# The last dense half of expert 0 as two more pairs of the Strassen passes

## The chip, the cores and the metric

The kernel runs on one core of a Trainium2 chip. The metric is the device time of one execution in microseconds; for the kernel before it is the median of three runs. TensorE does the matmuls into PSUM, VectorE, ScalarE and GpSimd the elementwise work, and SyncE issues nearly all transfers from one queue. In the profile they are called PE (PEld: its weight loads), DVE, ACT, POOL and SP.

## What is computed

Strided sparse attention over 4 batches, 8 heads, 576 positions and a head size of 64 gives x of 2304 tokens by 512. A mixture of 8 experts follows, in which every token goes through every expert; the gate is a Sinkhorn iteration over all tokens, so that no gate is known before the last token's logits.

```python
logits = x @ w_gate
P = np.exp(logits - logits.max())
for _ in range(8):
    P /= P.sum(1, keepdims=True) + 1e-09
    P /= P.sum(0, keepdims=True) + 1e-09
    P *= N / E
for e in range(E):
    h = np.maximum(x @ w1[e], 0.0)        # 512 -> 1024
    out += P[:, e:e + 1] * (h @ w2[e])    # 1024 -> 512
```

All of it is in float32. The kernel splits each operand of the experts' matmuls into a high and a low part and takes three products (high by high, high by low, low by high).

## The kernel before

**Dense phase.** Expert 0 is computed without the gate, since the gate isn't known yet. Its 1024 hidden columns are two F halves (`u` = 0 and 1, `UPE` = 2) of four tiles of 128 each (`FH` = 4, `ft`). A slot is one group of tokens by one `ft`: `layer1` makes twelve matmuls into `ph` and `rectify` the high part on ACT and the low part on DVE; `layer2` of the slot before follows and accumulates `y` over the four `ft`. The first half has 9 groups of 256 tokens, that is slots 0 to 35, and the attention's steps lie in slots 0 to 26. The second half has groups of 512, 512, 256, 512 and 512 tokens, slots 36 to 55. After the first half `y` is copied by ACT into `acc` (18 tiles of 128 tokens in `acc` and `tail`), after the second it is added by DVE, and the tiles from 6 on are stored to `yd` in DRAM. The layers 2 of the last two slots (`rest`) stand in step 0 of the passes.

**What lies beside the dense phase.** `store_x` writes x to `xd` in DRAM. `beside` gives the slots from 27 on their other work by a table: the logits (`gate_logits`, tile `pl`; `gate_transpose`, `pg`), the start of the gate (`pm`) and eight Sinkhorn rounds (`sinkhorn`: DVE row sums and a scaling, column sums `g8`, the matmul `pc` on PE, a second scaling on DVE); the sums of x for all three passes (`build_s`, read from `xd`, added on POOL, split by ACT and DVE, stored to `sd`); the operands of the first two pairs (`prep_w1`); and the scaling of `acc` by expert 0's gate (`scale`, on ACT).

**The passes.** The other experts are computed in three passes over 768 tokens each, by Strassen's scheme with seven products in the first layer: `step(g)` works on pair `g`, that is one tile of 128 hidden columns of either half of an expert, with x's blocks and their sums (`x11`, `x12`, `x22`, `s1` to `s4`) loaded into `reg`, over x's old place. There are `NK` = 28 pairs per pass. Pass 1 prepares the weights (`prep_w1` on POOL and ACT, `prep_w2` and `w2_sums` on DVE and ACT) and stores them to `wd` and `w2d`, and its second layer is ordinary (`second`, 36 matmuls); passes 2 and 3 load them back and have seven products in the second layer as well (`second_strassen`, 42 matmuls), but for one and two pairs at their ends. `step(g)` ends pair g-1: its last two products come first (`finish_first`), then five products of pair g, then the second layer of g-1.

Every engine runs its instructions in the order in which the code records them. So a wait of one instruction holds up all that stand behind it on its engine, and a DMA that waits for its buffer holds up the DMAs behind it on SP.

Of the kernel before, what the change touches and what calls it, by code (L numbers as in the profile page):

```python
# [55 lines left out]
def kernel(  # L56
# [35 lines left out]
    stacks = {"tail": ExitStack()}  # L92
    tail_p = stacks["tail"].enter_context(tc.tile_pool(name="tail", bufs=1))
# [17 lines left out]
    LATE = range(12, 16)  # L111
    EARLY = [t for t in range(HEAD, NTT) if t not in LATE]
    acc = big.tile([P, HEAD + len(LATE), D], F32, name="acc")
# [12 lines left out]
    tail = tail_p.tile([P, len(EARLY), D], F32, name="tail")  # L126
# [27 lines left out]
    plain = [(u, ft, which) for u in range(UPE) for ft in range(FH) for which in range(2)]  # L154
    plain[: 2 * FH] = sorted(plain[: 2 * FH], key=lambda x: x[2])
    plain[2 * FH :] = sorted(plain[2 * FH :], key=lambda x: (x[0], x[1] + 1.5 * x[2]))
# [288 lines left out]
    def layer2(u, c, ft, only=None):  # L445
# [8 lines left out]
        for i in range(nt) if only is None else only:  # L454
# [6 lines left out]
            if ft == FH - 1:  # L461
                t = c0 // P + i
                if t in EARLY:
                    o = tail[:, EARLY.index(t), :]
                else:
                    o = acc[:, t if t < HEAD else HEAD + t - LATE[0], :]
# [27 lines left out]
    for name in ("s3", "x22", "s4", "x12"):  # L494
        x_at[name] = at
        at += XN
    assert x_at["x12"] == 4 * 2 * NDT * CH and at <= 2 * NDT * NT
# [10 lines left out]
    NK = (E - 1) * FP  # L508
# [18 lines left out]
    def build_s(p, k):  # L527

        st = pools["sb"].tile([P, 4, 2, TN], F32, tag="sx", name=f"sx_{p}_{k}", bufs=2)
        t0 = 2 * TN * p  # L530
        for i, (dh, th) in enumerate(((0, 0), (0, 1), (1, 1), (1, 0))):
            nc.sync.dma_start(
                st[:, i], xd[:, :, k + 2 * dh, t0 + TN * th : t0 + TN * (th + 1)]
            )
        yield
        x, s = st[:, :, 0, :], st[:, :, 1, :]
        for i in (0, 2):
            nc.gpsimd.tensor_tensor(
# [759 lines left out]
```

## Time and profile before

| | us |
|---|---|
| median of 3 runs | 1563.97 (1562.67 to 1566.0) |
| the profiled execution | 1562.6 |
| its span, first to last instruction | 1560.8 |
| busy: TensorE | 1545.4 |
| busy: VectorE | 1270.2 |
| busy: GpSimd | 970.6 |
| busy: ScalarE | 536.6 |

The busy time of an engine counts the time in which at least one of its instructions runs, waits for a shared port among it. The granted clock of TensorE is full throughout. In the span the first F half's slots begin near 31 us, the second half's at 190.8, step 0 at 289.0, and the second layer of pass 2's first pair at 743.

### The profile page before, as it was taken

The numbers are of one execution on the slowest core, as the hardware profiler recorded it, in microseconds if no ns is written. First come the engines' busy times: TensorE is split into PE (matmuls) and PEld (weight loads), VectorE is DVE, ScalarE is ACT, GpSimd is POOL, SyncE is SP. The second block draws the span as 40 slices with busy tenths as digits, with TensorE's granted clock in tenths as the row PEclk, the third lists the DMA queues.
The fourth block names the chain that finished last, engine by engine and source line by source line (L and its number), as shares of the span: only waits on it lengthen the run. The fifth ranks groups of instructions, "written<-read, shape, count | busy, mean of one in ns | idle before, by whom it ended". The sixth has DMA issues, their size and how long they took to land.

```text
span 1560.8 us, 25458 instructions
## 1 busy us (share of the span) xinstructions
PE 1545.4 (99%) x9146; PEld 1452.1 (93%) x9146; DVE 1270.2 (81%) x2457; ACT 536.6 (34%) x1261; POOL 970.6 (62%) x899
## 2 busy tenths in 40 slices
PE   8999999999999999999999999999999999999999
PEld 6888888899999999989999999999999999999997
DVE  5655266699999999997688888888868888888887
ACT  6665322334343434342432222222232332222221
POOL 4221456365665565561777777777867877877874
PEclk9999999999999999999999999999999999999999
DMA  7553667988898888887866666666756766766762
GB/s 223 193 164 110 232 212 272 326 314 323 319 331 314 333 315 327 305 324 279 330 270 264 276 261 243 271 267 245 286 213 271 292 257 253 283 246 249 280 239 92
DMA packets 116766, 413.82 MB, mean 265 GB/s; under 512 B 9280, under 2 KB 63392, under 8 KB 102688
## 3 DMA queue, kind: packets, MB, share of 16 engines
q1 hardware_dynamic: 116496, 412.06, 70.0%
q8 instruction: 73, 1.20, 0.3%
q14 instruction: 53, 0.43, 0.1%
q10 hardware_dynamic: 144, 0.13, 0.0%
HBM read 275.27 MB, written 136.89 MB: 264 GB/s over the span
## 4 chain that ended last, share of the span: by engine, by line
PE 96%; DVE 1%; DMA 1%; POOL 0%; ACT 0%; issue 0%; DVEq 0%; POOLq 0%; ACTq 0%
PE p L827 25%; PE bb L697 17%; PE yg L726 16%; PE ba L697 11%; PE bc L697 11%; PE ph L424 6%; PE y L457 6%; PE tp L289 1%; DMA qk<-in_qkv 1%; PE sc L241 1%; PE pv L302 1%; PE pl L352 1%; PE sc L224 0%; PE pv L316 0%; PE tr L857 0%; POOL sm L277 0%
## 5 line engine op out<-in xcount | busy, mean ns | idle before, releaser
L835 DVE TENSOR_TENSOR total<-p,total 128x384 f32<-128x384 f32 x714 | 371.6, 557 | 0.8 <-PE p L827 0.8
L697 PE MATMUL bb<-reg 128*128 128x384 f32 x1512 | 304.3, 335 | 1.1 <-DVE u L750 0.7
L697 PEld LDWEIGHTS bb<-reg 128*128 128x128 f32 x1512 | 266.0, 188 | 4.1 <-DVE u L750 1.0
L697 PE MATMUL ba<-reg 128*128 128x384 f32 x1008 | 201.8, 334 | 0.6 <-DVE u L750 0.6
L697 PE MATMUL bc<-reg 128*128 128x384 f32 x1008 | 201.8, 334 | 0.0
L750 DVE TENSOR_TENSOR u<-bb,m 128x384 f32<-128x384 f32 x168 | 93.3, 555 | 106.3 <-PE bb L697 102.9
L808 ACT ACTIVATE a<-u 128x384 fp32r<-128x384 f32 x106 | 55.7, 526 | 359.4 <-DVE u L802 359.3
L697 PEld LDWEIGHTS ba<-reg 128*128 128x128 f32 x1008 | 177.2, 188 | 1.0 <-DVE u L750 0.9
L697 PEld LDWEIGHTS bc<-reg 128*128 128x128 f32 x1008 | 177.4, 188 | 0.0
L884 POOL TENSOR_TENSOR s1t<-m,u 128x384 f32<-128x384 f32 x53 | 53.9, 1017 | 189.3 <-DVE m L802 189.3
L733 DVE SCALAR_TENSOR_TENSOR acc<-yg,gate,acc 128x512 f32<-128x512 f32 x186 | 131.4, 741 | 9.6 <-PE yg L726 9.6
L726 PE MATMUL yg<-w2t,h 128*128 128x512 f32 x504 | 117.1, 390 | 0.0
L726 PE MATMUL yg<-w2b,h 128*128 128x512 f32 x504 | 117.1, 390 | 0.0
L827 PE MATMUL p<-s,w2b 128*128 128x384 f32 x648 | 116.7, 334 | 0.0
L424 PE MATMUL ph<-reg,w 128*128 128x256 f32 (+1 forms) x672 | 114.6, 318 | 0.0
L827 PEld LDWEIGHTS p<-s,w2b 128*128 128x128 f32 x648 | 112.7, 188 | 0.0
L827 PE MATMUL p<-s,w2t 128*128 128x384 f32 x624 | 112.3, 334 | 0.0
L457 PE MATMUL y<-w2t,h 128*128 128x512 f32 x432 | 111.0, 398 | 1.3 <-DVE acc L470 0.9
L726 PEld LDWEIGHTS yg<-w2b,h 128*128 128x128 f32 x504 | 94.4, 188 | 19.1
L726 PEld LDWEIGHTS yg<-w2t,h 128*128 128x128 f32 x504 | 94.4, 188 | 19.1
L812 POOL TENSOR_TENSOR a<-u,a 128x384 fp32r<-128x384 f32 x106 | 109.0, 1029 | 0.0
L827 PEld LDWEIGHTS p<-s,w2t 128*128 128x128 f32 x624 | 108.5, 188 | 0.0
(147 smaller groups left out, 2847.3 us busy)
## 6 DMA issues: line engine op xcount, KB each, us to landing
reg<-wd SPq DMA_DIRECT2D x52, 1792.0 KB
wd<-reg SPq DMA_DIRECT2D x28, 1792.0 KB
w2b<-w2d SPq DMA_DIRECT2D x25, 1792.0 KB
w2t<-w2d SPq DMA_DIRECT2D x24, 1792.0 KB
w2d<-w2b SPq DMA_DIRECT2D x14, 2048.0 KB
w2d<-w2t SPq DMA_DIRECT2D x14, 2048.0 KB
raws<-in_w SPq DMA_DIRECT2D x72, 256.0 KB
sx<-xd SPq DMA_DIRECT2D x24, 384.0 KB
```

The costliest lines, as they stand in the source:

```text
L241: nc.tensor.matmul(scs[j][:m, i, :m], t[sl, i * m : (i + 1) * m], t[sl, nq + i * m : nq + (i + 1) * m], start=True, stop=True,)
L424: nc.tensor.matmul(ph[:, :n], w[:, i, dt, :], xv(x, dt, c0, n), start=(first and len(taken) == 1 and i + x == 0), stop=(len(taken) == NDT ...
L457: nc.tensor.matmul(y, h[:, a, i * P : (i + 1) * P], w[:, b, :], start=(ft == 0 and first), stop=(ft == FH - 1 and a == 1),)
L697: nc.tensor.matmul(out[:, :TN], w[:, i, k, :], xops[x][:, xi, k, :], start=(start and n == 0), stop=(n == 5), skip_group_check=True,)
L726: nc.tensor.matmul(y, hg[g, i // 3, f][:, a, o : o + P], w[:, b, f, :], start=(f == 0 and a + b == 0), stop=(f == 1 and a == 1),)
L733: nc.vector.scalar_tensor_tensor(acc[:, i, :], y, gate[:, t, e : e + 1], acc[:, i, :], op0=ALU.mult, op1=ALU.add)
L750: nc.vector.tensor_tensor(o, bank[:, :TN], s, op=ALU.add)
L808: nc.scalar.activation(t[:, 0], src, AF.Copy)
L812: nc.gpsimd.tensor_tensor(t[:, 1], src, t[:, 0].bitcast(F32), op=ALU.subtract)
L827: nc.tensor.matmul(y[:, :TN], w[:, b, wi, d, :], h[:, a, :], start=(a + b == 0), stop=(a == 1),)
L835: nc.vector.tensor_tensor(o, y[:, :TN], o, op=ALU.add)
L884: nc.gpsimd.tensor_tensor(s1, m1, u3, op=ALU.add)
```

## The change

The second F half of expert 0 leaves the dense phase. Its four tiles of 128 hidden columns become two more pairs, pair (0, 2) and (1, 3), with expert index 0, so `NK` is 30; `f_at` gives the place of their columns in W1 and W2. The dense phase has slots 0 to 35 alone. With it go `tail`, the additions of `y` on DVE and the weight loads of that half; ACT copies each `y` to `acc` or, from tile 6 on, to one of four staging tiles that are stored to `yd`.

The work that stood beside the second half has new places:

- the logits' first three groups stand in slots 6 and 7, 13 and 14, 20 and 21, the other two in slots 27 and 28, the start of the gate in 28 and 29, and the Sinkhorn rounds in slots 29 to 35; the last round's matmul and second scaling stand after step 0, and the scaling of `acc` behind them
- the sums of x are built in pieces of 128 tokens instead of 384. Those of pass 1 (six pieces) are read from `reg` itself in slots 8 to 22; those of passes 2 and 3 (twelve pieces) are built in steps 3 to 27 of pass 1 (`later_sums`), one `next` per step, with the subtraction on POOL instead of DVE
- the raw weights of the first pair are loaded in slot 9 and prepared in slots 23 to 26, those of the second are loaded in slot 27 and prepared in slots 29 to 32

```diff
-    plain = [(u, ft, which) for u in range(UPE) for ft in range(FH) for which in range(2)]
...
+    plain = [(0, ft, which) for which in range(2) for ft in range(FH)]
...
-                if u == 0:
+                if t < HEAD:
+                    nc.scalar.activation(acc[:, t, :], y, AF.Copy)
+                else:
+                    o = acc[:, HEAD + t % STAGE, :]
                     nc.scalar.activation(o, y, AF.Copy)
-                else:
-                    nc.vector.tensor_tensor(o, y, o, op=ALU.add)
-                    if t >= HEAD:
-                        nc.sync.dma_start(yd[:, t - HEAD, :], o)
+                    nc.sync.dma_start(yd[:, t - HEAD, :], o)
...
-    NK = (E - 1) * FP
+    FE = (UPE - 1) * FH // 2
+    NK = (E - 1) * FP + FE
...
-            groups.append((p, 1 + k // FP, k % FP, k))
+            groups.append((p, (1 + k // FP) % E, k % FP, k))
...
+    def f_at(g, fh):
+        _, e, j, _ = groups[g]
+        return (FP * fh + j if e else FH + FE * fh + j) * P
...
+        t0 = 2 * TN * p + P * th
+        if p:
+            for i, (dh, t) in enumerate(((0, t0), (0, t0 + TN), (1, t0 + TN), (1, t0))):
+                nc.sync.dma_start(st[:, i], xd[:, :, k + 2 * dh, t : t + P])
+            yield
...
+        else:
+            for o, t in ((x[:, 0:4:3], t0), (x[:, 1:3], t0 + TN)):
+                ci, c = divmod(t, CH)
+                hi, lo = (
+                    chunk(ci)[:, i, k : k + 3 : 2, c : c + P].bitcast(F32) for i in range(2)
+                )
+                nc.gpsimd.tensor_tensor(o, hi, lo, op=ALU.add)
...
+        engine = nc.gpsimd if p else nc.vector
+        engine.tensor_tensor(so[:, 1], s, so[:, 0].bitcast(F32), op=ALU.subtract)
...
+    for n, (k, th) in enumerate((k, th) for k in range(2) for th in range(3)):
+        w = build_s(0, k, th)
+        for i in ((8, 9, 9), (10, 11, 11), (12, 15, 15), (16, 17, 17), (18, 19, 19), (19, 22, 22))[n]:
+            at(i, next, w, None)
+    w1_first = [prep_w1(g) for g in range(2)]
+    for g, i, pieces_at in ((0, 9, (23, 24, 25, 26)), (1, 27, (29, 30, 31, 32))):
+        at(i, load_w1g, g)
+        for n in pieces_at:
+            at(n, next, w1_first[g], None)
+    for i, name in (
+        (23, "x11"), (24, "s2"), (25, "s1"), (32, "x12"), (32, "s3"), (33, "x22"), (35, "s4"),
+    ):
+        at(i, load_x, 0, name)
+    at(27, load_w1g, 2)
+    at(33, load_w2g, 0)
+    for i, n in ((27, 1), (28, 2), (29, 1), (30, 1), (31, 1), (32, 1), (33, 1), (34, 1), (35, 1)):
+        for _ in range(n):
+            at(i, next, gat, None)
+    ahead_of_second = {28: 2, 29: 1, 35: 1}
...
+        for _ in range(ahead_of_second.get(slot, 0)):
+            next(gat, None)
...
+        elif slot in (6, 7, 13, 14, 20, 21):
             next(gat)
...
+            if g == 0:
+                assert next(gat, gat) is gat
+                for i in range(HEAD):
+                    scale(0, i)
             if g == 4:
                 gate_rows()
+            if g > 2:
+                next(later, None)
```

**PE around the last slots.** Before, a Sinkhorn round's `pc` has a whole slot of 512 tokens (`ph`, then four tiles of `y`) behind it; the rows end with step 0's first products (`ba`, `bb`):

```order
L389 MATMUL pc_3525<-g_7_3477,ones 128x8
L424 MATMUL ph_1536_2_3531<-reg,w_1_2_2697 128x512 x12
L457 MATMUL y_1536_0_3495<-w2t,h_1536_1_3492 128x512 x3
L457 MATMUL y_1536_1_3496<-w2t,h_1536_1_3492 128x512 x3
L457 MATMUL y_1536_2_3497<-w2t,h_1536_1_3492 128x512 x3
L457 MATMUL y_1536_3_3498<-w2t,h_1536_1_3492 128x512 x3
L424 MATMUL ph_1536_3_3564<-reg,w_1_3_2738 128x512 x12
L697 MATMUL ba_3609<-reg 128x384 x6
L697 MATMUL bb_3610<-reg 128x384 x6
```

After, in slots 34 and 35 and the start of step 0:

```order
L420 MATMUL ph_2048_2_2858<-reg,w_0_2_312 128x256 x12
L453 MATMUL y_2048_0_2834<-w2t,h_2048_1_2831 128x512 x3
L453 MATMUL y_2048_1_2835<-w2t,h_2048_1_2831 128x512 x3
L385 MATMUL pc_2880<-g_4_2856,ones 128x8
L420 MATMUL ph_2048_3_2893<-reg,w_0_3_365 128x256 x12
L385 MATMUL pc_2909<-g_5_2891,ones 128x8
L385 MATMUL pc_2923<-g_6_2920,ones 128x8
L692 MATMUL ba_2957<-reg 128x384 x6
L692 MATMUL bb_2958<-reg 128x384 x6
L692 MATMUL bc_2959<-reg 128x384 x6
L692 MATMUL ba_2957<-reg 128x384 x6
L453 MATMUL y_2048_0_2834<-w2t,h_2048_2_2871 128x512 x3
```

Slot 35 has a first layer alone, and the pc of two rounds follow each other behind it; `y` of the last two slots comes four products later, as before.

**ACT from the last slots to step 1.** Before, with the scaling of `acc` (`acc<-acc,gate`) in slots 54 and 55, the `w2b` rows of step 0 and the copy `m_1` of step 1:

```order
L1090 ACTIVATE acc<-acc,gate 128x512 x3
L439 ACTIVATE h_1536_3_3577<-ph_1536_3_3564 128x512
L1090 ACTIVATE acc<-acc,gate 128x512 x3
L181 ACTIVATE reg<-raws 128x256
L919 ACTIVATE m_0_3606<-ba_3609 128x384
L758 ACTIVATE h_0_3638<-ba_3609 128x384
L685 ACTIVATE w2b<-raws 128x1024
L653 ACTIVATE w2b<-w2sum_3643 128x1024
L758 ACTIVATE h_0_3688<-u_0_3608 128x384
L758 ACTIVATE h_0_3706<-m_0_3606 128x384
L758 ACTIVATE h_0_3715<-u_0_3607 128x384
L919 ACTIVATE m_1_3719<-ba_3722 128x384
```

After, from step 0's copy `m_0` to step 1's first weights (`ra`):

```order
L914 ACTIVATE m_0_2954<-ba_2957 128x384
L753 ACTIVATE h_0_2986<-ba_2957 128x384
L680 ACTIVATE w2b<-raws 128x1024
L648 ACTIVATE w2b<-w2sum_2991 128x1024
L463 ACTIVATE acc<-y_2048_0_2834 128x512
L463 ACTIVATE acc<-y_2048_1_2835 128x512
L753 ACTIVATE h_0_3020<-u_0_2956 128x384
L1111 ACTIVATE acc<-acc,gate 128x512 x6
L753 ACTIVATE h_0_3050<-m_0_2954 128x384
L753 ACTIVATE h_0_3059<-u_0_2955 128x384
L914 ACTIVATE m_1_3063<-ba_3066 128x384
L177 ACTIVATE reg<-ra_2590 128x512
```

All six scalings stand behind step 0's last relu, ahead of the two relus with which step 1 begins and of its copy `m_1`; two copies of `y` are new in step 0.

**SP around the raw weights of the second pair.** Before, from the load of `x12` into `reg` to the raw weights of the third pair:

```order
L574 DMA reg<-xd 128x4x384
L634 DMA wd<-reg 128x3584
L594 DMA raws<-in_w 128x2x128 x4
L562 DMA sd<-so_1_0_3367 128x2x384 x2
L472 DMA yd<-tail 128x512 x4
L562 DMA sd<-so_1_2_3368 128x2x384 x2
L594 DMA ra_3517<-in_w 128x2x128 x2
L594 DMA rb_3518<-in_w 128x2x128 x2
```

After, from the last two stores of x (slot 26) to the loads of slot 32:

```order
L149 DMA xd<-reg 1024x1x512
L149 DMA xd<-reg 1024x1x256
L629 DMA wd<-reg 128x3584
L589 DMA raws<-in_w 128x2x128 x4
L589 DMA ra_2590<-in_w 128x2x128 x2
L589 DMA rb_2591<-in_w 128x2x128 x2
L464 DMA yd<-acc 128x512 x4
L629 DMA wd<-reg 128x3584
L569 DMA reg<-xd 128x4x384
L565 DMA reg<-sd 128x1536
```

The raw weights (`raws<-in_w`) stand behind the last two stores of x and the store of the first pair's operands (`wd`); before, a load of x and that store stood ahead of them.

## Rows read from the trace of the kernel before

**Rows 1.** Page, part 1: busy us, share of the span, instructions of each engine.
```profile
PE 1545.4 (99%) x9146; PEld 1452.1 (93%) x9146; DVE 1270.2 (81%) x2457; ACT 536.6 (34%) x1261; POOL 970.6 (62%) x899
```

**Rows 2.** Timeline of PE, first F half: start us, us, instructions [idle before <-releaser].
```profile
53.55 0.56 PE L224 MATMUL sc<-qk 64*64 64x96 f32 x16 [1.18 <-DMA qk<-in_qkv]
...
156.45 1.59 PE L424 MATMUL ph<-reg,w 128*128 128x256 f32 x12
157.88 1.55 PE L457 MATMUL y<-w2t,h 128*128 128x512 f32 x6
...
162.63 1.99 PE L352 MATMUL pl<-reg,wgs 128*128 128x512 f32 x8
```

**Rows 3.** Timeline of PE, second F half.
```profile
206.01 2.88 PE L424 MATMUL ph<-reg,w 128*128 128x512 f32 x12
208.73 2.89 PE L457 MATMUL y<-w2t,h 128*128 128x512 f32 x12
...
240.88 1.62 PE L457 MATMUL y<-w2t,h 128*128 128x512 f32 x6 [0.94 <-DVE acc L470]
```

**Rows 4.** Timeline of PE, steps 0 and 1 and the second layer of the next.
```profile
288.96 1.22 PE L697 MATMUL ba<-reg 128*128 128x384 f32 x6
...
301.23 1.31 PE L697 MATMUL bb<-reg 128*128 128x384 f32 x6 [0.68 <-DVE u L750]
...
308.62 8.36 PE L726 MATMUL yg<-w2b,h 128*128 128x512 f32 x36
...
324.13 8.36 PE L726 MATMUL yg<-w2t,h 128*128 128x512 f32 x36
```

**Rows 5.** Timeline of PE, two pairs of pass 2, first product of each.
```profile
765.75 1.20 PE L697 MATMUL bb<-reg 128*128 128x384 f32 x6
...
780.32 1.20 PE L697 MATMUL bb<-reg 128*128 128x384 f32 x6
```

**Rows 6.** Timeline of DVE: a Sinkhorn round alone, and one beside GpSimd's sums.
```profile
211.78 0.17 DVE L391 TENSOR_SCALAR r<-pc 128x8 f32<-128x8 f32 x1
...
212.90 0.18 DVE L382 TENSOR_SCALAR g<-g 128x18 f32<-128x18 f32 x1
...
213.75 0.44 DVE L386 TENSOR_REDUCE g<-gate 128x8 f32<-128x144 f32 x1
...
258.41 0.17 DVE L391 TENSOR_SCALAR r<-pc 128x8 f32<-128x8 f32 x1 [1.53 <-PE pc L389]
...
259.53 1.36 DVE L382 TENSOR_SCALAR g<-g 128x18 f32<-128x18 f32 x1
...
262.15 0.44 DVE L386 TENSOR_REDUCE g<-gate 128x8 f32<-128x144 f32 x1
```

**Rows 7.** Timelines of SP's queue and ACT; windows with DMA share and GB/s last.
```profile
155.86 1.25 SPq L151 DMA_DIRECT2D xd<-reg  x2
...
157.00:165.00 8.00, 8.00 (x50) 6.85 (x49) 1.41 (x4) 1.97 (x4) 0.00 (x0) 1.00 1.04 380
...
268.28 0.33 SPq L634 DMA_DIRECT2D wd<-reg  x1
...
275.94 0.63 ACT L181 ACTIVATE reg<-raws 128x512 fp32r<-128x512 f32 x1 [2.99 <-DMA raws<-in_w]
```

**Rows 8.** Timeline of ACT, last slots to step 1.
```profile
284.74 1.94 ACT L1090 ACTIVATE acc<-acc,gate 128x512 f32<-128x512 f32 x3
...
298.35 1.06 ACT L653 ACTIVATE w2b<-w2sum 128x1024 fp32r<-128x1024 f32 x1 [2.87 <-DVE w2sum L652]
...
304.66 0.49 ACT L919 ACTIVATE m<-ba 128x384 f32<-128x384 f32 x1
```

**Rows 9.** Pass 1: windows (busy of PE, PEld, DVE, ACT, POOL; clock, DMA, GB/s) and timeline.
```profile
402.00:464.00 62.00, 62.00 (x313) 56.25 (x312) 59.64 (x82) 25.02 (x44) 35.83 (x29) 1.00 0.87 320
446.20:447.40 1.20, 1.20 (x8) 1.20 (x8) 0.97 (x1) 1.14 (x2) 1.20 (x1) 1.00 1.10 332
...
440.11 1.40 DVE L652 TENSOR_TENSOR w2sum<-w2sum,raws 128x256 f32<-128x256 f32 x1
```

More of the change, by code (lines that the diff above doesn't have):

```diff
@@ L110 @@
     HEAD = 6
-    LATE = range(12, 16)
-    EARLY = [t for t in range(HEAD, NTT) if t not in LATE]
-    acc = big.tile([P, HEAD + len(LATE), D], F32, name="acc")
+    STAGE = 4
+    acc = big.tile([P, HEAD + STAGE, D], F32, name="acc")
     raws = buf.tile([P, 4 * D], F32, name="raws")
@@ L122, in raw_slots @@
         return raws[:, o : o + n * D]
-    tail = tail_p.tile([P, len(EARLY), D], F32, name="tail")
     CH = 4 * P
@@ L493 @@
     at += W1N
-    for name in ("s3", "x22", "s4", "x12"):
+    for name in ("x12", "s3", "x22", "s4"):
         x_at[name] = at
         at += XN
-    assert x_at["x12"] == 4 * 2 * NDT * CH and at <= 2 * NDT * NT
+    assert x_at["s4"] == 4 * 2 * NDT * CH and at <= 2 * NDT * NT
     wops = [
@@ L1092, in scale @@
         )
[L1094 to L1135 removed]
+    slots = [(0, (c, 2 * P), ft) for c in range(0, NT, 2 * P) for ft in range(FH)]
     prev = None
[L1137 to L1138 removed]
+    for slot, (u, c, ft) in enumerate(slots):
         busy = at_k < NS + LAG
@@ L1144 @@
             layer1(u, c, ft)
-        if last and u + 1 < UPE:
-            split_w(u + 1, ft, 0)
+        for _ in range(ahead_of_second.get(slot, 0)):
+            next(gat, None)
         if slot == 1:
-            layer2(*prev[:3])
+            layer2(*prev)
         if busy:
@@ L1162 @@
             split_gate()
-        elif slot == 22:
+        elif slot in (6, 7, 13, 14, 20, 21):
             next(gat)
@@ L1172 @@
                 store_x()
-                open_pools("right", ("sb", 1))
-                work = beside(gat)
-        else:
-            for x in work.get(slot - len(slots) + 20, ()):
-                x()
-        prev = (u, c, ft, last)
-    assert next(gat, gat) is gat
-    for name in ("s3", "x22", "s4"):
-        load_x(0, name)
-    for _ in w1_first[1]:
-        pass
+                open_pools("right", ("hg", 8))
+        for x in work.get(slot, ()):
+            x()
+        prev = (u, c, ft)
+    for x in w1_first:
+        for _ in x:
+            pass
     stacks["left"].close()
-    stacks["tail"].close()
+    stacks["sums"].close()
     w2b = ctx.enter_context(tc.tile_pool(name="w2b", bufs=1, side="left"))
@@ L1190, with later_sums @@
     pools["u"] = ctx.enter_context(tc.tile_pool(name="u", bufs=2, side="left"))
-    open_pools("left", ("rab", 1))
+    open_pools("left", ("rab", 1), ("sb", 1))
+    def later_sums():
+        for p in range(1, NPASS):
+            for k in range(2):
+                for th in range(3):
+                    w = build_s(p, k, th)
+                    next(w)
+                    yield
+                    next(w)
+                    yield
+                    for _ in w:
+                        pass
+    later = later_sums()
     for g in range(NG + 1):
```

99 lines of the change are left out of this document (22 added, 77 removed).

## Prediction

> **What bounds the kernel now.** I read the busy times first: TensorE is at work for 1545.4 of 1560.8 us, VectorE for 1270.2 [rows 1]. So the time is TensorE's work plus its waits, and what has to be found is how much matmul time the change takes out and which new waits it puts in. Next I read TensorE in order of time, stretch by stretch. In the slots of the first F half a slot of 256 tokens is a layer 1 of 1.43 us (156.45 to 157.88) and a layer 2 of about the same; a matmul group for logits takes about 2 [rows 2]. In the second F half a layer 1 over 512 tokens takes 2.72 us, and a layer 2 the same; one wait of 0.94 stands there [rows 3]. A pair in pass 1 takes 15.51 us, start to start of its second layers [rows 4]; one in pass 2 takes 14.57, which is 14 products of 1.04 [rows 5]. Between these stretches nothing is idle, so whole blocks can be subtracted and added. Then I read the engines beside TensorE for the work that moves: VectorE for one Sinkhorn round [rows 6], SP's queue and ScalarE for the weight loads [rows 7], ScalarE for the scaling of acc [rows 8], VectorE and the DMA engines in pass 1 [rows 9].
>
> **The change part by part.**
>
> *Matmuls removed.* The second half of expert 0 has 16 slots of 512 tokens and 4 of 256: 32 x 2.72 for the first kind (layers 1 and 2), 8 x about 1.40 for the second: 98.2 us. Its waits go too: 0.94 there [rows 3], 0.68 in step 0 [rows 4], two shorter ones, some 3 us with the restarts behind them.
>
> *Matmuls added.* Two pairs in each of three passes: 2 x 15.51 in pass 1, 4 x 14.57 in passes 2 and 3 (what ends a pass differently is counted from its end and stays): 31.0 + 58.3 = 89.3 us. Logits and Sinkhorn matmuls only move. Sum so far: -98.2 - 3.0 + 89.3 = -11.9.
>
> *An early wait that goes.* At 53.55 TensorE waits 1.18 us for a qk load [rows 2]. That load stands on SP behind the first store of x, and that store behind a load of second-half weights, which waited for its buffer. These loads are gone. Bounds 0 and -1.2; I take -1.2, since nothing else holds the store up. Sum: -13.1.
>
> *The Sinkhorn rounds in short slots.* Each round is: pc matmul, eight small VectorE operations, next pc. TensorE takes its queue in order, so a pc whose column sums aren't ready holds everything behind it. A round takes 2.41 us on VectorE from 211.78 to the end at 214.19, with GpSimd idle, and 4.18 from 258.41 to 262.59 beside GpSimd's sums: the small TENSOR_SCALAR takes 0.18 in the first and 1.36 in the second [rows 6]. From pc to pc that is 2.7 and 4.5. A slot of 512 tokens lasted 5.4 and hid either; a slot of 256 lasts 2.8 to 3.1. The rounds now stand in slots 30 to 35.
> - The end. Slot 35 has no layer 2 (its two last ones go into step 0): the order gives layer 1, pc, pc, first product. The first pc of the two has 1.6 us of cover against 2.7: wait 1.1. The second has none: 2.7. GpSimd is idle by then. 3.8 us, and I see nothing that hides it.
> - The start. The raw weights of the second pair are asked for in slot 27, on SP behind two stores of x (3 MB) and the store of the first pair's operands. In the kernel before, the x stores are issued at 155.86 and fill the DMA engines from 157 to 165; a store of the operands issued at 268.28 lets ScalarE start on the raw weights behind it at 275.94, 7.7 later [rows 7]. Queued behind x: 165 plus about 7, less the issue, is 172, which is 15.5 after slot 27's start (156.45). ScalarE's copy of them (0.63, rows 7) stands ahead of the relu of slot 30; VectorE's low half stands behind that relu, and the first round's operations behind the low half. So that round starts at about 17.0 instead of 15.4, and GpSimd then has the second pair's seven operations and the third pair's first three, some 10 us. With 4.18 it ends at 21.2; its pc is reached at 18.2: wait 3.0. For the two rounds after it, partly beside GpSimd, I take 1.0 and 1.9. Bounds for the three together: 1.3 (GpSimd's operations miss the small ones) and 8 (every round at 4.18, weights 2 us later). I take 5.9, since GpSimd's work is there without a gap.
>
> The rows say that a small operation is held up for part of a GpSimd operation, 1.77 us for the three of a round that can be [rows 6]. The Trainium skill, page "SBUF — State Buffer", section "Who interferes with whom", says that a VectorE instruction with two SBUF inputs and a GpSimd one shut each other out for a whole instruction, while a TENSOR_REDUCE is never held; by that all three operations with two such inputs would be held as long as the TENSOR_SCALAR was. The trace agrees with which operations are held, not that all are held so long, and I stay with the rows; what the rule would do is in rival 3.
>
> *Scaling of acc after step 0.* Before, six scalings (1.94 for three, rows 8) lay in the last dense slots, where ScalarE is idle. Now the last round's pc stands behind step 0's last product and the scalings behind it, ahead of step 1's two relus and its copy of the first product, for which the product w21 waits. Chain in step 0, from its first product: in the kernel before, ScalarE's copy of the W2 sums starts at 298.35, 9.4 after 288.96 [rows 4, 8]; without the waits ahead of it 8.7. Then that copy 1.06, two y copies 1.2 (they are VectorE additions in the kernel before), a relu 0.5, its low half 0.6, the end of the last round 0.7: 12.8 to 13.0. Scalings 3.8, two relus and the copy 1.4 (the copy alone is 0.49, rows 8): 18.1. TensorE would be at w21 at 13.4: five products and y 2.8, a pc, six products. Wait 4.7. Bounds 3 and 6.5.
>
> *Sums of x.* For pass 1 they read reg directly, with no transfer: six builds in slots 8 to 22, where GpSimd and VectorE have room. The logits pairs there put one more PSUM tile between transposes. Bounds 0 and 2; I take 0.5. For passes 2 and 3 they stand in pass 1, whose VectorE is busy for 59.64 of 62 us [rows 9], but their subtraction is on GpSimd. GpSimd's new operations stand just ahead of those that now hold up VectorE's W2 sums (1.40 at 440.11 for 256 columns, rows 9), and are shorter or, every second step, wait for ScalarE; so VectorE should not get slower. ScalarE's copy of 512 columns (0.6) every second step falls before the next relu. DMA: 1 MB more every second step, in pieces of 512 bytes; such a stretch moves 332 GB/s, so 3.2 us in 31 us. The share of 0.87 at 320 GB/s becomes about 0.97 [rows 9]. Bounds 0 and 15 us; I take 0.5, since loads are asked for a step ahead.
>
> The highest rate of the rows is 380 GB/s over 8 us [rows 7]; pass 1 would need 354. The Trainium skill, page "DMA: Bandwidth & Descriptors", section "Specifications", gives about 358 GB/s as a core's limit to HBM. By it pass 1 would be at the limit and the rival on DMA below the likeliest; the trace goes above that figure, so I don't raise its chance for it.
>
> *Sum.* Waits 3.8 + 5.9 + 4.7 = 14.4, the two small ones 1.0: -13.1 + 15.4 = +2.3 us. The profiled execution is 1562.6 with a span of 1560.8; the median is 1563.97. On the median: 1566.3, and I say 1566.
>
> **The rivals.**
> 1. Faster. The waits at the start of the rounds stay near their lower bound (1.3 instead of 5.9) because GpSimd's and VectorE's operations fall beside each other: +2.3 - 4.6 = -2.3, and with the scalings at their lower bound -4.0: 1560. For it: half of a round's operations can't be held up at all. Against it: the row of 4.18 is from a like stretch. 0.22.
> 2. Slower, through DMA in pass 1. Each second step 3.2 us more are queued; if a store of W2 operands then lands after ScalarE wants to write the next ones into that buffer, ScalarE and with it the relu before the second layer is late. It decides once the queue stands more than some 5 us behind. Price at 0.4 to 0.8 us in each of 12 steps: 5 to 10, on top of the sum: 1571 to 1576. For it: share 0.97. Against it: the idle that is left recovers each step's lag. 0.15.
> 3. Slower, in the slots. Each of the three small operations of a round that can be held waits as long as the one of rows 6, 1.36 - 0.18 = 1.18, so 3.5 a round where I count 1.77; over three rounds that is +5.3. Or the raw weights come 2 us later: +2. For it: GpSimd has some 10 us of operations without a gap. Against it: the row of 4.18 was measured beside such a stretch. 1568 to 1572. 0.20.
> That the blocks don't add up as said I put in the forecast's width: they are counted matmuls.
>
> **How the numbers follow.** Forecast 0.43, its own range 1561 to 1567; rivals 0.22, 0.15, 0.20. A measurement of this kernel can tell 0.2% (3.1 us) from no change. The range over all: from 1559 (rival 1 and the lower bounds of the scalings) to 1573 (rivals 3 and most of 2). Faster 0.22, same 0.43, slower 0.35.
>
> **What would show it.** In the profile after: TensorE's busy time down by some 9 us; two pc matmuls behind each other with waits of 1.1 and 2.7 ahead of the first product of step 0; a wait for the round in slots 31 to 33; ScalarE's six scalings between two relus and a wait of TensorE in step 1; no wait near 53 us; pass 1 at 15.5 us a pair. If the pairs of pass 1 are longer than 15.6, rival 2 holds; if the waits in slots 31 to 33 are under 2 us together, rival 1. I'm wrong altogether if the first slots, where I read no new wait, hold one.

## The result and the profile after

The changed kernel takes 1582.58 us (median of four runs, 1582.12 to 1586.01) against 1564.11 of the kernel before: ratio 1.0122, 95% interval 1.0104 to 1.014. It is slower by 18.5 us, where I had forecast 2 and had let the range end at 1573.

The page of the profiled execution (1586.01 us, span 1584.2): busy time, share and instructions by engine, and the chain of work that ended last.

```profile
PE 1551.0 (98%) x9182; PEld 1459.8 (92%) x9182; DVE 1315.3 (83%) x2545; ACT 548.3 (35%) x1293; POOL 1050.0 (66%) x1033
...
PE 69%; DVE 12%; DMA 5%; POOL 5%; issue 3%; ACT 3%; SPq 3%; POOLq 0%; ACTq 0%; DVEq 0%
```

TensorE should have been at work for 9 us less than in [rows 1] and is at work for 5.6 more. DVE and POOL now stand in the chain with 12% and 5% (1% and 0% in the kernel before). To find where, I laid the starts of the second layers of pass 1 side by side. In the kernel before they are 15.51 apart, but for one step of 15.61 and the last of 15.54. After the change the 22 steps from 303.47 to 662.60 us take 16.32 on average, and these are 22 of the 24 steps in which GpSimd makes the sums for passes 2 and 3; the first two with sums still take 15.61 and 15.63. The steps ahead of them take 15.51, but for the very first, 16.34, in which TensorE's clock is down (last section); those behind them take 15.50 and 15.53. 22 x 0.81 is 17.9 us, nearly all of the loss. Passes 2 and 3 take 14.57 a pair, as in [rows 5].

TensorE in two of these steps (timeline: start, us, instructions, idle before and its releaser):

```profile
447.67 1.20 PE L692 MATMUL ba<-reg 128*128 128x384 f32 x6
449.23 1.32 PE L692 MATMUL bb<-reg 128*128 128x384 f32 x6 [0.35 <-DVE u L745]
450.39 8.36 PE L721 MATMUL yg<-w2b,h 128*128 128x512 f32 x36
...
463.81 1.21 PE L692 MATMUL ba<-reg 128*128 128x384 f32 x6
465.57 1.33 PE L692 MATMUL bb<-reg 128*128 128x384 f32 x6 [0.56 <-DVE u L745]
466.75 8.36 PE L721 MATMUL yg<-w2t,h 128*128 128x512 f32 x36
```

TensorE's waits of this kind in the whole execution (us in total, times, longest):

```profile
PE bb L692 <- DVE u L745: 10.6, 23, 0.9
```

The product t3 goes into bank bb, which VectorE's addition u must have read. That addition is late in every one of the 22 steps; the 23rd wait, of 0.89, stands ahead of step 1. Beside a wait the products also start further apart (465.57 to 466.75 is 1.18, where the others are 1.04 apart), which makes 0.8 of a wait of 0.35 to 0.56. What VectorE, ScalarE and GpSimd did ahead of the second of these waits, in the changed kernel:

```profile
459.42 1.06 ACT L648 ACTIVATE w2t<-w2sum 128x1024 fp32r<-128x1024 f32 x1 [3.05 <-DVE w2sum L647]
460.39 0.61 ACT L550 ACTIVATE so<-sx 128x512 fp32r<-128x512 f32 x1
...
461.08 1.29 POOL L553 TENSOR_TENSOR so<-sx,so 128x512 fp32r<-128x512 f32 x1 [2.44 <-ACT so L550]
462.33 1.29 POOL L617 TENSOR_TENSOR rt<-rb,ra 128x512 f32<-128x512 f32 x1
463.70 0.94 POOL L620 TENSOR_TENSOR ru<-ra,rt 128x256 f32<-128x256 f32 x1
...
461.75 0.55 DVE L745 TENSOR_TENSOR u<-bc,u 128x384 f32<-128x384 f32 x1
462.43 1.61 DVE L757 SCALAR_TENSOR_TENSOR h<-m,h 128x384 fp32r<-128x384 f32 x1
463.96 1.09 DVE L757 SCALAR_TENSOR_TENSOR h<-u,h 128x384 fp32r<-128x384 f32 x1
464.97 0.55 DVE L745 TENSOR_TENSOR u<-bb,m 128x384 f32<-128x384 f32 x1
```

The same place in the kernel before:

```profile
439.75 1.48 POOL L622 TENSOR_TENSOR rt<-rb,ra 128x512 f32<-128x512 f32 x1
...
442.19 0.74 POOL L626 TENSOR_TENSOR ru<-rb,ru 128x256 f32<-128x256 f32 x1
445.95 2.38 POOL L182 TENSOR_TENSOR reg<-ra,reg 128x512 fp32r<-128x512 f32 x1 [3.02 <-ACT reg L181]
...
444.54 0.56 DVE L762 SCALAR_TENSOR_TENSOR h<-m,h 128x384 fp32r<-128x384 f32 x1
445.02 0.55 DVE L762 SCALAR_TENSOR_TENSOR h<-u,h 128x384 fp32r<-128x384 f32 x1
445.48 0.55 DVE L750 TENSOR_TENSOR u<-bb,m 128x384 f32<-128x384 f32 x1
```

The two relu lows (h from m, h from u, both inputs in SBUF) took 0.56 and 0.55 while GpSimd was idle from 442.93 to 445.95. After the change GpSimd makes its differences of raw weights (rt, ru, ru) right beside them. The first relu low starts 0.1 behind rt, and ends at 464.04, 0.42 after rt's end at 463.62; the second ends 0.41 after that of the first ru. Each is held until the GpSimd operation is through. The relu low of the third quarter, whose input is in PSUM, stays at 0.56 (467.65 us). The Trainium skill, page "SBUF — State Buffer", section "Who interferes with whom", has this as an exclusive lock on a shared port: whoever issues first keeps it for the whole instruction, and a VectorE instruction with two SBUF inputs meets it. The rows agree.

Why GpSimd is late there stands in the same rows: its subtraction so waits 2.44 us for ScalarE's copy so, which stands behind ScalarE's copy of the W2 sums. That is a theory until runs tell it apart from others.

The profiled execution has one thing that the other three runs of the changed kernel probably lack. At 95.36 us TensorE waits 1.8 us for a qk load, and in the windows from 96 to 100 us its granted clock is 0.73 and 0.50. That is some 3.3 us, with the 1.6 by which the work behind it up to the next transposes takes longer than in run 7's trace. The profiled execution is 3.3 to 3.9 us above the others (1582.12 to 1582.71), whose mean clock is 0.998 against its 0.997; they have no trace that would show it.

### The profile page after: what moved, and what is told of

It is laid out like the page before. It is cut to its first block, busy times and chain, and to the rows that moved or that the text cites. A ratio compares the mean times of both kernels' runs of the same rounds, so it can differ in the third digit from the quotient of the medians.

```text
span 1584.2 us, 25846 instructions
## 1 busy us (share of the span) xinstructions
PE 1551.0 (98%) x9182; PEld 1459.8 (92%) x9182; DVE 1315.3 (83%) x2545; ACT 548.3 (35%) x1293; POOL 1050.0 (66%) x1033
## 4 chain that ended last, share of the span: by engine, by line
PE 69%; DVE 12%; DMA 5%; POOL 5%; issue 3%; ACT 3%; SPq 3%; POOLq 0%; ACTq 0%; DVEq 0%
PE p L822 26%; PE bb L692 13%; PE ba L692 8%; PE bc L692 8%; PE yg L721 4%; DMA raws<-in_w 3%; DVE acc L728 3%; PE y L453 2%; PE ph L420 2%; POOL reg L178 2%; DVE u L745 2%; DVE w2t L682 2%; DVE w2b L682 2%; SPq L527 2%; DVE h L757 1%
## 5 line engine op out<-in xcount | busy, mean ns | idle before, releaser
L830 DVE TENSOR_TENSOR total<-p,total 128x384 f32<-128x384 f32 x770 | 400.7, 557 | 0.8 <-PE p L822 0.8
L692 PE MATMUL bb<-reg 128*128 128x384 f32 x1620 | 330.1, 338 | 10.6 <-DVE u L745 10.6
L692 PEld LDWEIGHTS bb<-reg 128*128 128x128 f32 x1620 | 285.2, 188 | 20.4 <-DVE u L745 17.9
L692 PE MATMUL ba<-reg 128*128 128x384 f32 x1080 | 217.6, 336 | 2.5 <-ACT m L914 2.2
L692 PE MATMUL bc<-reg 128*128 128x384 f32 x1080 | 217.2, 335 | 0.0
L692 PEld LDWEIGHTS ba<-reg 128*128 128x128 f32 x1080 | 190.5, 189 | 3.1 <-ACT m L914 2.5
L692 PEld LDWEIGHTS bc<-reg 128*128 128x128 f32 x1080 | 189.4, 188 | 2.2 <-ACT h L753 2.2
L721 PE MATMUL yg<-w2b,h 128*128 128x512 f32 x540 | 126.3, 392 | 0.0
L745 DVE TENSOR_TENSOR u<-bc,u 128x384 f32<-128x384 f32 x180 | 99.6, 553 | 4.1 <-PE bc L692 1.0
L178 POOL TENSOR_TENSOR reg<-rt,reg 128x512 fp32r<-128x512 f32 x28 | 36.3, 1297 | 94.1 <-ACT reg L177 94.1
```

The source lines that it names most:

```text
L178: nc.gpsimd.tensor_tensor(lo, src, hi.bitcast(F32), op=ALU.subtract)
L692: nc.tensor.matmul(out[:, :TN], w[:, i, k, :], xops[x][:, xi, k, :], start=(start and n == 0), stop=(n == 5), skip_group_check=True,)
L721: nc.tensor.matmul(y, hg[g, i // 3, f][:, a, o : o + P], w[:, b, f, :], start=(f == 0 and a + b == 0), stop=(f == 1 and a == 1),)
L745: nc.vector.tensor_tensor(o, bank[:, :TN], s, op=ALU.add)
L830: nc.vector.tensor_tensor(o, y[:, :TN], o, op=ALU.add)
```

## The experiments

All times are medians; the kernel before had 1563.5, 1564.08, 1562.89 and 1564.16 in the four groups of runs.

**1. Transfers or GpSimd?** The sums' work on GpSimd is left out for passes 2 and 3; every transfer and ScalarE's copies stay (the store of the low parts sends the high parts, with the same bytes).

```diff
             yield
-            for i in (0, 2):
-                nc.gpsimd.tensor_tensor(
-                    x[:, i : i + 2], x[:, i : i + 2], s[:, i : i + 2], op=ALU.add
-                )
...
-            nc.gpsimd.tensor_tensor(s[:, i, :], a, b, op=op)
+            if not p:
+                nc.gpsimd.tensor_tensor(s[:, i, :], a, b, op=op)
...
-        engine.tensor_tensor(so[:, 1], s, so[:, 0].bitcast(F32), op=ALU.subtract)
+        if not p:
+            nc.vector.tensor_tensor(so[:, 1], s, so[:, 0].bitcast(F32), op=ALU.subtract)
```

> Left out: all GpSimd work of the six sums of x for each of passes 2 and 3 (the two additions, four sums and the subtraction), so those sums are not computed; their loads, ScalarE copies and stores, with all bytes, stay in pass 1. Theory A (GpSimd's new work pushes its weight differences beside VectorE's two relu lows, each of which waits for a GpSimd operation to end): the 22 steps of 16.3 us in pass 1 go back to 15.5, 22 x 0.8 = 17.6 us less than the changed kernel's 1582.6: 1565, and the two relu lows back at 0.56 us. Theory B (rival 2 of the prediction, the DMA queue of pass 1): nothing changes, 1582, steps at 16.3.

Measured 1565.04 us, ratio 1.0012 (1.0002 to 1.0021). Pass 1 between 400 and 650 us in this run (window: busy of PE, PEld, DVE, ACT, POOL; clock, DMA share, GB/s):

```profile
400.00:650.00 250.00, 250.00 (x1259) 226.72 (x1258) 240.23 (x324) 105.20 (x185) 145.55 (x112) 1.00 0.95 355
```

The relu lows from u are back at 0.555 us on average there (32 of them), from 0.824 in the changed kernel. The DMA engines are at 0.95 and 355 GB/s, higher than the 0.92 and 340 of the changed kernel in the same window, and TensorE never stops. Rival 2 of the prediction is out.

**2. GpSimd's operations alone, in the kernel before.** They work on scratch tiles, at the same place and in the same shapes.

```diff
+    def dummy(n):
+        x, s = sx[:, :, 0, :], sx[:, :, 1, :]
+        if n % 2:
+            nc.gpsimd.tensor_tensor(so[:, 1], s, so[:, 0], op=ALU.subtract)
+            return
+        for i in (0, 2):
+            nc.gpsimd.tensor_tensor(
+                x[:, i : i + 2], x[:, i : i + 2], s[:, i : i + 2], op=ALU.add
+            )
+        for i in range(4):
+            nc.gpsimd.tensor_tensor(s[:, i], x[:, i], x[:, 3 - i], op=ALU.subtract)
...
+            if 2 < g < 27:
+                dummy(g - 3)
```

> The kernel before, with operations on GpSimd alone added on two scratch tiles behind steps 3 to 26, in turn two additions and four sums, then one subtraction, in the shapes of the changed kernel and at its place in the program; no transfer, no ScalarE copy, nothing reads the results. Theory A: 22 to 24 steps grow from 15.51 to 16.3, 18 to 19 us: 1582 to 1583 against 1564.1 of the kernel before. Theory B (DMA): no change, 1564.

Measured 1565.63 us, 1.0015 (1.0006 to 1.0025): only 2 us more. Theory A as I had stated it fell: neither the transfers nor the same GpSimd work makes the loss by itself. GpSimd in a step with the subtraction:

```profile
455.76 1.47 POOL L1200 TENSOR_TENSOR so<-sx,so 128x512 f32<-128x512 f32 x1
457.19 1.48 POOL L622 TENSOR_TENSOR rt<-rb,ra 128x512 f32<-128x512 f32 x1
...
459.57 0.74 POOL L626 TENSOR_TENSOR ru<-rb,ru 128x256 f32<-128x256 f32 x1
```

Here nothing waits for ScalarE. GpSimd goes from its last split straight to the subtraction and is through with the differences at 460.31, ahead of the relu lows at 460.54. The steps with the additions and four sums do run into them, but this lag is made good in the next step, so only four of the 24 steps take 15.96 or 15.97.

**3. The same with ScalarE's copy ahead of the subtraction.** Still no transfer.

```diff
         if n % 2:
+            nc.scalar.activation(so[:, 0], s, AF.Copy)
             nc.gpsimd.tensor_tensor(so[:, 1], s, so[:, 0], op=ALU.subtract)
```

> The kernel before with the scratch operations on GpSimd as in the run that added them alone, and now ScalarE's copy of 512 columns ahead of the subtraction, on scratch too, at the end of a step where it stands behind the copy of the W2 sums; still no transfer. Theory A2 (GpSimd's subtraction waits for that copy, so the weight differences behind it start some 3 us later and fall beside the two relu lows in every second step, which then makes GpSimd late in the step between): 22 to 24 steps at 16.3, 1581 to 1583. Theory B2 (the load of x sums by the DMA queue is needed too): as without the copy, 1565.6.

Measured 1579.41 us, 1.0102 (1.0086 to 1.0118). That is a little under theory A2's 1581. One copy of 0.61 us in every second step, on an engine that is busy for a third of the time, makes 14 us against run 2. ScalarE, GpSimd and VectorE in this run:

```profile
462.97 1.06 ACT L653 ACTIVATE w2b<-w2sum 128x1024 fp32r<-128x1024 f32 x1 [3.05 <-DVE w2sum L652]
463.93 0.61 ACT L1200 ACTIVATE so<-sx 128x512 f32<-128x512 f32 x1
...
464.62 1.29 POOL L1201 TENSOR_TENSOR so<-sx,so 128x512 f32<-128x512 f32 x1 [2.44 <-ACT so L1200]
465.88 1.29 POOL L622 TENSOR_TENSOR rt<-rb,ra 128x512 f32<-128x512 f32 x1
...
465.97 1.62 DVE L762 SCALAR_TENSOR_TENSOR h<-m,h 128x384 fp32r<-128x384 f32 x1
467.51 1.09 DVE L762 SCALAR_TENSOR_TENSOR h<-u,h 128x384 fp32r<-128x384 f32 x1
```

It is the changed kernel's pattern to a hundredth: 2.44 us of waiting, relu lows of 1.62 and 1.09. Twenty steps take 16.16 to 16.37. Nothing is made good here, because the steps between, with the additions and sums, hold the relu lows as well (1.03 and 1.09 at 417.66 and 418.62).

**4. The copy moved, in the changed kernel.** ScalarE's copy so goes to the middle of a step; the subtraction stays at its end.

```diff
                     next(w)
                     yield
+                    next(w)
+                    yield
                     for _ in w:
                         pass
...
+            if 4 < g < NK and g % 2:
+                next(later, None)
             if not strassen(g):
                 relu_hi(g, 1, 1, u3)
```

> The changed kernel with one thing moved in pass 1: ScalarE's copy of the sums stands in the middle of a step, ahead of the relu of the fourth quarter, and GpSimd's subtraction stays at the step's end, where it now waits for nothing. Additions, sums, transfers and their places stay. Theory A2: the weight differences are through before the relu lows in every second step, so the lag of the steps with sums is recovered: steps of 15.5 with some of 16.0, 1565 to 1569. Rival A (any sums at the step's end push the weight differences beside the relu lows): 1582. Rival B2: 1582.

Measured 1566.57 us, 1.0023 (1.0013 to 1.0032): 16 us come back from moving one copy. GpSimd:

```profile
450.22 1.26 POOL L178 TENSOR_TENSOR reg<-rb,reg 128x256 fp32r<-128x256 f32 x1
451.44 1.47 POOL L553 TENSOR_TENSOR so<-sx,so 128x512 fp32r<-128x512 f32 x1
452.86 1.48 POOL L617 TENSOR_TENSOR rt<-rb,ra 128x512 f32<-128x512 f32 x1
```

The subtraction follows the split at once. Of the 29 steps of pass 1, 23 take 15.50 or 15.51; four of the others, 15.80 to 16.05, lie in the stretch of the sums. Runs 2, 3 and 4 together name the cause: the wait of GpSimd's subtraction for a copy that stands behind ScalarE's copy of the W2 sums. With the wait the loss is there without any transfer, and without the wait it is gone with every transfer in place.

**5. All of the later sums in the middle of a step.**

```diff
+            if 2 < g < NK:
+                next(later, None)
             if not strassen(g):
                 relu_hi(g, 1, 1, u3)
...
-            if g > 2:
-                next(later, None)
```

> The changed kernel with the work on the later sums called in the middle of a step, behind the operands' second piece (GpSimd idle for 3.3 us there in the trace) instead of at its end. All bytes and operations stay. Theory A: the weight differences return to where they stood in the kernel before, the relu lows to 0.56; what is left is VectorE's subtraction of 1024 columns and the third relu low beside the sums, at most 0.3 us a step: 1565 to 1572. Theory B (DMA): 1582.

Measured 1564.41 us, 1.0007 (0.9995 to 1.0019), a little under what I expected at the lower end: all steps of pass 1 take 15.51, but for the first (15.66) and the one of 15.61 that the kernel before has too. The same operations and bytes fit into GpSimd's idle time in the middle of the step. VectorE is still held, but in other instructions (its subtraction of 1024 columns takes 1.7 to 1.9 there, as in the kernel before, its sums of W2 over 1.0), and it gets that back before TensorE asks for the next addition u. So the rest of the change costs about 1 us.

**6. Is it only that one addition?** In the changed kernel, u goes ahead of the two relu lows on VectorE.

```diff
-        elif not turning(G) or not new:
+        elif not new:
             for x in late:
                 relu_lo(G, *x)
...
-            if turning(G):
+            if not s:
                 for x in late:
                     relu_lo(G, *x)
```

> The changed kernel with one swap on VectorE: the addition u behind the product t2 goes ahead of the two relu lows in every step of pass 1 (and the last ones of the others that go the same way); GpSimd's operations, ScalarE's copy and the transfers stay as in the changed kernel, so the weight differences still fall beside the relu lows. Theory F (what costs is the lateness of that one addition, for which the product t3 waits, and not VectorE's share of busy time): the waits of 0.32 to 0.58 us go, steps of 15.5 to 15.7, 1565 to 1570, with the relu lows still at 0.9 to 1.6 us. Rival G (VectorE has no room for the held time at all): the second layer or a later addition waits instead, steps stay at 16.2 or more, 1580 to 1583.

Measured 1591.33 us, 1.0175 (1.0159 to 1.0192): worse. Theory F's time did not come; the steps take 16.1 to 16.8, but for one of 15.97 and the last of 15.54, about as rival G had it, and the time is above G's. But the swap costs by itself: the steps that start at 238.68 and 255.28 us, ahead of GpSimd's first operation on the later sums (280.9), already take 16.60 and 16.83. VectorE in the second of these, VectorE in a step with sums, and TensorE:

```profile
269.71 0.56 DVE L745 TENSOR_TENSOR u<-bb,m 128x384 f32<-128x384 f32 x1 [0.97 <-ACT m L914]
...
467.16 1.13 DVE L757 SCALAR_TENSOR_TENSOR h<-m,h 128x384 fp32r<-128x384 f32 x1
...
459.05 3.01 PE L721 MATMUL yg<-w2b,h 128*128 128x512 f32 x12 [0.37 <-DVE acc L728]
```

The wait ahead of t3 is gone, but the addition needs ScalarE's copy m, so VectorE now idles 0.97 us for it in every step, with sums or without, and its lateness comes out in the second layer, as a wait for acc. So a microsecond lost on VectorE's queue costs TensorE time at this place too; but the run does not part F from G, since the loss is there without GpSimd's sums. Whether the lateness of the one addition is all that costs stays open. VectorE's busy share does not show any of this: in the window from 400 to 650 us it is busy for 231.49 us in the changed kernel and for 241.10 in the kernel before, which is 15.1 and 15.0 us a step; time in which an instruction is held counts as busy, in both.

**7. The qk load.** The first pair's raw weights are asked for in slot 13.

```diff
-    for g, i, pieces_at in ((0, 9, (23, 24, 25, 26)), (1, 27, (29, 30, 31, 32))):
+    for g, i, pieces_at in ((0, 13, (23, 24, 25, 26)), (1, 27, (29, 30, 31, 32))):
```

> The changed kernel with the loads of the first pair's raw weights (1 MB in pieces of 512 bytes) asked for in slot 13 instead of slot 9. Theory C: these loads, ahead of the store of x and the qk load, hold the qk load for which TensorE waits 1.77 us at 95.4 us and runs at half clock for some us behind; both go, with 1.7 us of lost clock: 3.5 us less, 1579. Rival: the store of x (2 MB) holds the qk load by itself, as it did at 53.55 us in the kernel before: 1582 to 1583, the wait stays above 1 us.

Measured 1583.3 us, 1.0128 (1.0112 to 1.0144), no gain. TensorE's waits from 30 to 170 us in this run, the only group:

```profile
PE tp L285 <- DVE lt L352: 1.2, 2, 0.6
```

The wait is gone, but it was not in the median to begin with: without this edit, run 1 shows it with 0.5 us and run 5 not at all; in run 4's profiled execution (1569.75 us, 3.2 above its median) a qk load is waited for at 28.36 us, for 1.62. Neither side of my expectation held. What makes it come in one execution and not in another was not tried.

**8. The scalings, and the rounds.** On top of run 5, first the six scalings of acc alone, moved behind the relu of step 1's product w21; then also the last but one round moved into step 0, behind its third product, and the last one behind step 1's first product.

```diff
+            if g == 1:
+                for i in range(HEAD):
+                    scale(0, i)
...
-    ahead_of_second = {28: 2, 29: 1, 35: 1}
+    ahead_of_second = {28: 2, 29: 1}
...
             mul(g, "t1", "s1", bc, True)
+            if not g:
+                next(gat)
...
         mul(g, "t4", "x22", bb, False)
+        if not g:
+            assert next(gat, gat) is gat
```

> The run with the sums in the middle of a step (1564.4), and of the two repairs in steps 0 and 1 the scalings alone: behind the relu of step 1's product w21. The rounds stay in slot 35 and at the end of step 0. Theory D: the wait of 2.2 for the copy m and the half clock behind it (1.5) go, 3.7 us: 1560.7; the rest of the 7.9 us of the run with both, 4.2, is then the rounds'. Rival: both act on the same wait, and this one alone gives under 2 us: 1562.5 or more.

> Built on the run with the sums in the middle of a step (1564.4): the last but one round goes from slot 35 into step 0 behind its third product, the last round behind step 1's first product, and the six scalings of acc in step 1 behind the relu of its product w21, where ScalarE is idle for some 3.9 us. Theory D (each of these waits is cover that is missing, and the half clock behind the two long ones follows from them): the wait of 2.5 us ahead of step 0 goes with 1.6 of lost clock, the wait of 2.2 for the copy m in step 1 with 1.5: 6 to 8 us less, 1557 to 1559. Rival: the waits move to the next products of steps 0 and 1 (VectorE does the rounds between its own work there): less than 3 us gained, 1562 or more.

Measured: the scalings alone 1562.03 us, 0.999 (0.998 to 1.0); both 1556.47 us, 0.9952 (0.9938 to 0.9967). The first gives 2.4 us by medians, with intervals that overlap (run 5's is 0.9995 to 1.0019), and 3.9 by the two profiled executions (1564.37 and 1560.48). Of the 3.9, some 1.4 lie ahead of the product w21, where the edit moves nothing; what it takes away in the trace is the wait of 2.2. So its price is the wait alone, nearer to the rival than to theory D, whose half clock behind that wait is not in run 5's trace (last section). Both together give 7.9, as theory D had it. With both, the changed kernel is faster than the one before by 0.5%. TensorE's waits from 30 to 250 us in run 5, then with both:

```profile
PE pc L385 <- DVE g L382: 6.9, 5, 2.5
PE ba L692 <- ACT m L914: 2.2, 1, 2.2
PE tp L285 <- DVE lt L352: 1.2, 2, 0.6
PE bb L692 <- DVE u L745: 0.9, 1, 0.9
PE ba L692 <- DVE r L387: 0.3, 1, 0.3
```

```profile
PE pc L385 <- DVE g L382: 4.3, 4, 1.4
PE tp L285 <- DVE lt L352: 1.2, 2, 0.6
PE bb L692 <- DVE u L745: 1.2, 1, 1.2
```

The waits add up to 4.8 us less, and the gain is 7.9. Most of the difference is TensorE's clock; the last section has it.

**9. One more round in step 0,** and no round in slot 32; then, in a second kernel, the low half and the sums of W2 behind the additions u on VectorE. Both kernels also give the rounds' `pc` tiles another tag in PSUM (`s` for `t`), whose effect was not measured by itself.

```diff
-    for i, n in ((27, 1), (28, 2), (29, 1), (30, 1), (31, 1), (32, 1), (33, 1), (34, 1), (35, 1)):
+    for i, n in ((27, 1), (28, 2), (29, 1), (30, 1), (31, 1), (33, 1), (34, 1), (35, 1)):
...
                 for x, only in rest:
                     layer2(*x, only)
+                next(gat)
```

```diff
             if not g:
-                next(w2n, None)
-                next(w2n, None)
                 for x, only in rest:
                     layer2(*x, only)
...
             if not strassen(g):
                 relu_hi(g, 1, 1, u3)
+            if not g:
+                next(w2n, None)
+                next(w2n, None)
```

> As the run before it, but one round more goes into step 0 (behind its layer-2 products of the last slots) and slot 32 has none, so that the round behind it has two slots. Theory D: the waits of slots 31 to 35 (0.8, 1.1, 0.9, 0.9) fall to 2 us or less together: 1.5 to 2.5 us less than the run before it, 1555 to 1557. Rival: the rounds of steps 0 and 1 are late instead and the time is the same or longer.

> As the run with the rounds spread (1560.7), whose wait of 5.2 us for u came from VectorE's queue: in step 0 a round and the addition u stood behind the low half and the sums of W2, which wait for their raw weights. Here that low half and the sums of W2 stand behind the additions u. Theory E (order on VectorE): that wait falls under 2 us, and the time to 1554 to 1557, at or under the 1556.5 of the run with one round fewer in step 0. Rival: VectorE has no room for a second round in step 0 at all; the wait stays above 3 us, 1559 or more.

Measured 1560.66 us, 0.9977 (0.9967 to 0.9986), and 1556.09 us, 0.9953 (0.9937 to 0.997). The first has the waits in the slots down to 2.0 us as theory D said, and a new one of 5.2 ahead of step 1, as the rival said, so the gain did not come; in the windows from 205 to 215 us TensorE's clock is 0.66. VectorE there:

```profile
203.52 1.23 DVE L682 TENSOR_TENSOR w2b<-raws,w2b 128x1024 fp32r<-128x1024 f32 x1 [1.86 <-ACT w2b L680]
...
206.19 0.16 DVE L387 TENSOR_SCALAR r<-pc 128x8 f32<-128x8 f32 x1
...
208.48 0.55 DVE L745 TENSOR_TENSOR u<-bb,m 128x384 f32<-128x384 f32 x1
```

The low half of W2 waits for ScalarE's high half, and that for the raw weights; the round and u stand behind it. With that order changed the wait is 1.8 us, as theory E said, but the time is no better than with one round fewer in step 0.

## Why the prediction was wrong

The step that failed is the second half of *Sums of x*: "VectorE should not get slower", 0.5 us taken, 17.9 in the trace and 18.2 between the changed kernel and run 5. The argument looked at GpSimd's new operations where they stand, and compared their length with that of the operations which hold VectorE's W2 sums. It did not follow what they push back. Two things in it were half seen. That they "every second step, wait for ScalarE" was in the text, but its length was not worked out, though the rows had it: in [rows 8] ScalarE's copy of the W2 sums waits for VectorE until 9.4 us into step 0, and the copy so stands behind it. And that ScalarE's copy "falls before the next relu" asked only whether ScalarE has time for it, not who waits for it. GpSimd's queue is in order, so the weight differences wait too, and come to stand beside the two relu lows, whose place between additions for which TensorE waits had too little slack to be held in step after step. I bounded this term with 0 and 15 us, took 0.5, and then let the range reach only to 1573: with the bound in it, it would have ended at 1581, still short of 1582.58.

The Trainium skill's rule on the lock was cited and set aside ("not that all are held so long, and I stay with the rows"), and used only for the Sinkhorn rounds. In pass 1 it decided.

Rival 2 had the right place and a size of 5 to 10 us, but the wrong mechanism: runs 1 and 3 show the loss without its cause and its cause without the loss. "If the pairs of pass 1 are longer than 15.6, rival 2 holds" was wrong as a test, since it tells only where, not why.

The other steps, by run 5, which has the rest of the change undisturbed:
- *Matmuls.* 15.51 and 14.57 a pair held. With both repairs of run 8, whose mean clock is 1.000, TensorE is busy for 1537.3 us, 8.1 less than [rows 1]; I had said some 9.
- *The early qk wait.* Right: the wait of [rows 2] is gone. But two waits for the logits' copy lt take its place (1.2 us together), where I had 0.5 for all sums and logits in the slots; a new wait in the first slots was among the signs of being wrong. Slot 27 starts at 162.47; 156.45 with two logits groups of 1.84 and three transposes of 0.35 moved ahead of it, less 1.2, is 160.0. So these slots cost 2.5 more than the sum without that term, half of it in waits that the trace shows and half that I can't place.
- *The rounds.* At the end of the slots 1.1 and 2.7 were forecast; in the changed kernel they are 0.9 and 2.5. At the start 5.9; the waits of slots 31 to 33 there are 2.8 us together (0.83, 1.07, 0.90), and 3.5 in run 5, about halfway between the lower bound of 1.3 and my 5.9. A round there takes 4.0 to 4.4 us from pc to pc, as [rows 6] had it; what failed is the late start, which I had put at 3.0 of wait for the first round, behind the raw weights, and which is 0.83 there and 1.46 in run 5.
- *The scalings.* 4.7 forecast, in the trace 2.2 for the copy m, and in the changed kernel some 1.6 more behind it. Both ends of that sum were off: in run 5 ScalarE's copy ends 19.6 us after step 0's first product, where I had 18.1, and TensorE comes to w21 after 17.4, where I had 13.4, having waited 1.2 and run part of step 0 at a lower clock. (The "six products" of the prediction are five by the order; 13.4 is worked out with five.)
- Not in the sum at all: the clock, below.

The terms apart from pass 1 came to +1.8 in the sum; run 5 is 0.9 above its runs of the kernel before. That sum came out right by luck, since its terms were off both ways.

## What to carry to other kernels

When work is added to a queue, follow what it pushes back: for each later operation there, ask beside whose instructions it will now run, and whether those have slack. An operation that waits for another engine costs its queue the whole wait, not its own length, so put what it waits for on that engine ahead of anything that waits long. Busy shares tell little here: in the window from 400 to 650 us VectorE was busy for less time than in the faster kernel, and ScalarE's part was 0.6 us at 35% load.

## What the runs showed of the hardware

TensorE's clock fell behind the longer waits, though in the kernel before its mean is 1.000. Windows of the changed kernel (clock, DMA share and GB/s last):

```profile
200.00:205.00 5.00, 2.53 (x10) 2.44 (x11) 3.85 (x15) 0.00 (x0) 0.00 (x0) 0.77 1.04 410
205.00:210.00 5.00, 5.00 (x25) 4.77 (x24) 1.55 (x4) 1.65 (x3) 0.00 (x0) 0.88 0.35 136
...
220.00:225.00 5.00, 3.08 (x13) 3.08 (x14) 3.89 (x5) 4.22 (x9) 2.54 (x2) 0.82 0.25 93
225.00:230.00 5.00, 5.00 (x20) 4.04 (x19) 4.90 (x7) 1.35 (x3) 1.70 (x2) 0.84 0.91 385
```

With both repairs of run 8, from 195 us on:

```profile
195.00:200.00 5.00, 4.06 (x26) 3.85 (x25) 4.38 (x15) 0.88 (x2) 0.00 (x0) 1.00 1.05 412
200.00:205.00 5.00, 5.00 (x28) 4.48 (x26) 4.38 (x11) 1.44 (x2) 0.00 (x0) 1.00 0.77 308
```

In the changed kernel TensorE waits 0.94 and 2.47 us just ahead of the first pair of windows, and 2.18 in the second; its first products behind them take 2.27 and 1.76 in place of 1.2, which is the level of 1.2 GHz in place of 2.4 for part of them. So the two long waits cost some 1.6 us more each there than they last. Behind waits of up to 1.36 us, with both repairs, the clock stays at 1.0.

The length of a wait alone does not decide it. Run 5 has the same waits of 0.94, 2.47 and 2.20, and these windows:

```profile
200.00:205.00 5.00, 5.00 (x18) 5.00 (x18) 2.71 (x9) 0.49 (x1) 0.00 (x0) 0.53 0.81 324
...
220.00:225.00 5.00, 5.00 (x26) 4.45 (x26) 5.00 (x5) 2.04 (x4) 3.53 (x2) 1.00 0.38 158
```

There the clock falls behind the first two only, from 195 us on (0.78, then 0.53), and for longer: the three products behind them start 2.07, 1.92 and 1.33 apart where others are 1.04, 2.2 us more in all, which is most of what run 8's gain has beyond the waits. Behind the wait of 2.20, which ends at 219.72, it is 1.00, and so it is behind one of 1.77 in the second kernel of run 9 (window from 205 to 210 us). What decides was not tried.

Two of these windows have the DMA engines at 410 and 412 GB/s over 5 us. In the prediction the limit to HBM of 358 GB/s (the Trainium skill, page "DMA: Bandwidth & Descriptors", section "Specifications") was set against a row of 380; these rows are further above it.
